# Moving the query chains of batches 4 and 5 to earlier half steps in a hand-ordered attention and highway kernel

## The chip, the cores and the metric

The kernel runs on one core of one Trainium2 chip. The metric is the time of one execution in device microseconds. Executions of one kernel differ by up to about 1 us either way.

Engines: PE is TensorE (PEld its weight loads), DVE VectorE, ACT ScalarE, POOL GpSimd, SP the engine that issues the transfers. L64 means line 64 of the kernel; L64 and L69 are helpers that issue all matmuls and all PE transposes, so groups are told apart by their tile names: `pq` query transposes, `psk` the kv product, `px` the attention output, `pt` and `ph` the two highway products, `nat` the output transposes. On the other engines `eq` and `ek` are the exps of queries and keys, `r` their sums and reciprocals, `qsT` the copied-out query transposes, `kvn` the normalised kv product (the "kv norm"), `dd` and `g` DVE's two steps of the highway layer, and `o` the output copies.

## The reference

Linear attention over 8 batches of 8 heads, 576 rows, 64 columns, followed by a highway layer on 512 columns:

```python
q_s = softmax(q, axis=-1)                    # over the 64 columns
k_s = softmax(k, axis=2)                     # over the 576 rows
kv  = einsum('bhsd,bhse->bhde', k_s, v)
x   = einsum('bhsd,bhde->bhse', q_s, kv)     # then heads side by side: 4608 x 512
H, T = relu(x @ w_h), sigmoid(x @ w_t + b_t)
out  = T * H + (1 - T) * x
```

## The kernel before

All instructions are issued by hand in one global order. Each engine executes its own instructions in that order, and in the traces a waiting instruction holds up those behind it: POOL of the kernel before idles 4.02 us in front of a scaling (57.79) though the data of the value casts behind it had landed by 53.0. The order is written as events at "half steps": `at(p, f)` puts `f` at position `p`, and the sorted events are emitted. Eight half steps make a slot. In the slot of batch b (it begins at p = 8(b-1)) the query chain of batch b ends on PE, while the highway layer of the batch before runs, one gate (`pt`) and one carry (`ph`) for each of four column blocks ("ob 0" to "ob 3"); chunk 2 is batch 2's highway work, and so on.

```python
def q_sums(b, a):                      # DVE: row sums of half a batch, 1152 elements a partition
    ...
    nc.vector.reduce_sum(qsum[b][:, :, h], eq[b][:, :, h, :], axis=AX.X)

def q_scale_p(b, n0, n1):              # POOL: exp times reciprocal of the sums
    e, r = eq[b][:, n0:n1], qsum[b][:, n0:n1]
    nc.gpsimd.tensor_mul(e, e, r.broadcast_to(list(e.shape)))

def q_trans(b, g, home=None):          # PE transposes into one PSUM bank, DVE copies out
    ...
    if home is None:
        home = ps_1.tile([P, 1024], FP16, tag="q1", name=f"pq_{b}_{g}")   # ps_1: a pool of one
    ...
    nc.vector.tensor_copy(qsT[b][:, :, n0:n1, :], t[:, :, 0:w, :])

# ... in the event list, for each batch b:
at(p + e0, E(exp_half, b, "q", 0))     # ACT
at(p + e1, E(exp_half, b, "q", 1))
at(p + s0, E(q_sums, b, 0))            # DVE
at(p + s1, E(q_sums, b, 1), E(q_recip, b))
at(p + sc, E(q_scale_p, b, 0, 4))      # POOL
```

A query's path is ACT (exp), DVE (sums, reciprocal), POOL (scaling), PE (transposes), DVE (copy `qsT`). And the second transpose of a batch cannot start before DVE has copied out the first, because the pool `ps_1` has one bank: in the kernel before, DVE's copy of batch 3's first starts at 50.78 and takes 0.69 us, and PE's second follows at 51.60.

The softmax here doesn't subtract the row's maximum and nothing guards it: scores larger than these inputs give would overflow.

## Time and profile before

| what | value |
|---|---|
| time, median of 3 runs | 132.03 us (132.03 to 132.52) |
| span of the profiled execution | 130.2 us |
| slot of batch 3, by first gate activations on ACT (45.90 to 57.53) | 11.6 us |
| slots of batches 4 and 5 | 12.6 and 13.3 us |
| slots of batches 6 and 7 | 11.2 and 10.5 us |
| PE stands in front of batch 4's second transpose | 0.81 us |
| PE stands in front of batch 5's first and third transpose | 0.92 and 0.78 us |

The last two rows of the table are from PE's timeline. Its columns are start, duration, engine, line, operation, output and input, count, and in brackets the idle time before it and what ended it:

```profile
62.04 0.62 PE L69 MATMUL pq<-ident,eq 128*128 128x128 f16 x8 [0.81 <-POOL eq L264]
71.06 0.62 PE L69 MATMUL pq<-ident,eq 128*128 128x128 f16 x8 [0.92 <-POOL eq L264]
74.97 0.27 PE L69 MATMUL pq<-ident,eq 128*128 128x128 f16 x2 [0.78 <-DVE qsT L282]
```

Twice PE waits for POOL's scaled queries, once for DVE's copy. Those stalls are what the change aims at. The stages and the chain are shown inside the prediction.

### The profile page before, as it was taken

How to read it: one execution, taken by the hardware profiler on the slowest of the kernel's cores; microseconds unless marked ns; L12 is line 12 of the kernel's file. 1: busy time of each engine (PE TensorE's matmuls, PEld its weight loads, DVE VectorE, ACT ScalarE, POOL GpSimd, SP SyncE). 2: the span in 40 equal slices, each digit the busy share in tenths (PEclk: the TensorE clock that was granted, in tenths of full speed). 3: DMA queues.
4: the chain of work that ended last, by engine and by line, in shares of the span. 5: the costliest groups of instructions: out<-in, count | busy, mean ns of one | idle time of the engine just before them, and what ended most of it. 6: DMA issues, size and time to landing. Idle time of an engine off the chain costs nothing.

```text
span 130.2 us, 3374 instructions
## 1 busy us (share of the span) xinstructions
PE 112.3 (86%) x1375; PEld 61.3 (47%) x1375; DVE 97.6 (75%) x179; ACT 92.6 (71%) x130; POOL 75.3 (58%) x71
## 2 busy tenths in 40 slices
PE   4999996986877999998997899989999999999810
PEld 1335442462334356444644464445555554788700
DVE  1396537797899999899698889769956566789920
ACT  3652159985998589779889956997994856657420
POOL 2006506790299999529947952994799535425400
PEclk9999999999999999999999999999999999999985
DMA  4999999999999999999999999999048406074991
GB/s 147 359 393 399 404 403 408 411 414 412 402 414 408 403 414 410 403 413 400 324 409 407 340 322 413 396 134 374 8 81 222 206 40 287 0 322 204 403 340 31
DMA packets 20584, 41.25 MB, mean 317 GB/s; under 512 B 5460, under 2 KB 5976, under 8 KB 19544
## 3 DMA queue, kind: packets, MB, share of 16 engines
q1 hardware_dynamic: 20568, 41.03, 84.6%
q8 instruction: 11, 0.18, 0.5%
q14 instruction: 5, 0.04, 0.1%
HBM read 30.41 MB, written 9.44 MB: 306 GB/s over the span
## 4 chain that ended last, share of the span: by engine, by line
PE 29%; DVE 20%; POOL 19%; DMA 11%; issue 7%; ACT 6%; SPq 3%; POOLq 0%; DVEq 0%; ACTq 0%
POOL eq L264 12%; DMA q<-in_q_dram 11%; PE ph L64 10%; PE pt L64 8%; DVE r L234 5%; DVE dd L401 5%; PE nat L64 4%; DVE g L409 4%; POOL g L420 4%; POOL v L195 3%; PE pq L69 3%; ACT eq L183 2%; SPq L96 2%; PE psk L64 2%; ACT w16h L116 1%
## 5 line engine op out<-in xcount | busy, mean ns | idle before, releaser
L264 POOL TENSOR_TENSOR eq<-eq,r 128x1024 f16<-128x1024 f16 (+2 forms) x16 | 29.8, 1876 | 15.2 <-DVE r L252 10.6
L64 PE MATMUL pt<-xT,w16t 128*128 128x512 f16 x128 | 34.0, 379 | 2.1 <-DVE dd L401 1.2
L64 PE MATMUL ph<-xT,w16h 128*128 128x512 f16 x128 | 33.4, 380 | 1.2 <-ACT w16h L116 0.8
L383 ACT ACTIVATE pt<-pt,bt 128x512 f32<-128x512 f32 (+1 forms) x40 | 24.7, 621 | 9.8 <-PE pt L64 9.3
L409 DVE SCALAR_TENSOR_TENSOR g<-pt,dd 128x512 f16<-128x512 f32 (+1 forms) x40 | 25.2, 633 | 3.4 <-DVE dd L401 0.5
L401 DVE SCALAR_TENSOR_TENSOR dd<-xT,ph 128x512 f16<-128x512 f16 x32 | 21.7, 679 | 6.4 <-PE ph L64 6.3
L420 POOL TENSOR_TENSOR g<-g,xT 128x512 f16<-128x512 f16 x19 | 21.7, 1157 | 5.7 <-DVE g L409 5.7
L64 PEld LDWEIGHTS <-w16t 128*128 128x128 f16 x160 | 14.8, 98 | 18.1 <-issue 5.2
L183 ACT ACTIVATE eq<-q 128x1152 f16<-128x1152 f32 x16 | 18.4, 1172 | 4.0 <-DMA q<-in_q_dram 4.0
L234 DVE TENSOR_REDUCE r<-eq 128x18 f32<-128x1152 f16 x12 | 16.2, 1346 | 4.6 <-ACT eq L183 4.5
L183 ACT ACTIVATE ek<-k 128x1152 f16<-128x1152 f32 x16 | 18.6, 1175 | 1.3 <-DMA k<-in_k_dram 1.3
L64 PEld LDWEIGHTS <-w16h 128*128 128x128 f16 x160 | 13.6, 98 | 11.6 <-ACT w16h L116 2.5
L195 POOL CAST v<-v 128x1152 f16<-128x1152 f32 x12 | 13.5, 1150 | 9.5 <-DMA v<-in_v_dram 9.5
L64 PE MATMUL nat<-ident,g 128*128 128x128 f16 x142 | 16.9, 219 | 1.2 <-ACT o L460 0.6
L64 PEld LDWEIGHTS <-g 128*128 128x128 f16 x144 | 13.2, 98 | 8.2 <-DVE g L409 1.1
L460 ACT COPY o<-nat 128x512 f32<-128x512 f32 x26 | 15.6, 601 | 0.0
L64 PE MATMUL warm<-wide,ident 128*128 128x512 f16 x41 | 12.2, 445 | 1.8 <-DVE wide L153 1.8
L354 ACT CAST xT<-px 128x1024 f16<-128x1024 f32 x10 | 10.2, 1017 | 4.9 <-PE px L64 4.9
L69 PE MATMUL pq<-ident,eq 128*128 128x128 f16 x104 | 8.5, 219 | 4.2 <-POOL eq L264 1.7
L282 DVE COPY qsT<-pq 128x1024 f16<-128x1024 f16 (+1 forms) x16 | 9.3, 588 | 1.9 <-PE pq L69 1.4
L69 PEld LDWEIGHTS <-eq 128*128 128x128 f16 x108 | 6.7, 97 | 7.7 <-POOL eq L264 2.6
L357 ACT CAST xT<-px 128x512 f16<-128x512 f32 x8 | 4.3, 591 | 8.2 <-PE px L64 8.2
(57 smaller groups left out, 107.8 us busy)
## 6 DMA issues: line engine op xcount, KB each, us to landing
out_dram<-o SPq DMA_DIRECT2D x8, 1024.0 KB, 4.8
q<-in_q_dram SPq DMA_DIRECT2D x7, 1152.0 KB, 13.5
k<-in_k_dram SPq DMA_DIRECT2D x7, 1152.0 KB, 13.2
v<-in_v_dram SPq DMA_DIRECT2D x5, 1152.0 KB, 13.8
v<-in_v_dram SPq DMA_DIRECT2D x6, 576.0 KB, 11.6
q<-in_q_dram SPq DMA_DIRECT2D x2, 576.0 KB, 3.9
k<-in_k_dram SPq DMA_DIRECT2D x2, 576.0 KB, 6.6
w32t<-in_moe_w_t_dram SPq DMA_DIRECT2D x1, 1024.0 KB, 10.3
```

Of the source, the lines that this page charges most:

```text
L64: mm = lambda o, l, r, st, sp: nc.tensor.matmul(o, l, r, start=st, stop=sp, skip_group_check=True)
L69: nc.tensor.matmul(o, i, ident, is_transpose=True, start=True, stop=True, skip_group_check=True,)
L183: nc.scalar.activation(dst[b][:, :, 2 * a : 2 * a + 2, :], in32[which][b][:, 2 * a : 2 * a + 2].rearrange("p c n d -> p n c d"), AF.Exp,)
L195: (eng or nc.gpsimd).tensor_copy(o, i)
L234: nc.vector.reduce_sum(qsum[b][:, :, h], eq[b][:, :, h, :], axis=AX.X)
L264: nc.gpsimd.tensor_mul(e, e, r.broadcast_to(list(e.shape)))
L354: copy[how](dst, t2.rearrange("p c (n d) -> p c n d", d=64))
L383: nc.scalar.activation(ps, ps, AF.Tanh, bias=bt2[:, ob : ob + 1], scale=0.5)
L401: nc.vector.scalar_tensor_tensor(dd, xv(ob), -0.5, ps, op0=ALU.mult, op1=ALU.max)
L409: nc.vector.scalar_tensor_tensor(gv(ob), th, 1.0, dd, op0=ALU.add, op1=ALU.mult)
L420: eng.tensor_add(gv(ob), gv(ob), xv(ob))
L460: nc.scalar.copy(o, flat(t))
```

## The change

The intent: the slots of batches 4 and 5 are longer than the later ones, and their query chains are placed later. So give them the later slots' half steps, let the scaled queries be ready sooner, and move the key exps, value casts, transposes, kv and x products to match. No operation is added or removed. The whole diff:

```diff
         if b > 2:
             e0, e1, s0, s1, sc = {
                 3: (-2.6, -1.6, -1.1, -0.1, 1),
-                4: (-5.5, -4.5, -2.8, -1.5, -1.4),
-                5: (-5, -4, -3.4, -2.7, -2.6),
-            }.get(b, (-6.6, -5.2, -5.5, -3.95, -3.9))
+                4: (-5.6, -4.4, -4.6, -3.0, -2.9),
+            }.get(b, (-6.6, -5.2, -5.4, -3.95, -3.9))
             at(p + e0, E(exp_half, b, "q", 0))
             at(p + e1, E(exp_half, b, "q", 1))
             at(p + s0, E(q_sums, b, 0))
             at(p + s1, E(q_sums, b, 1), E(q_recip, b))
             at(p + sc, E(q_scale_p, b, 0, 4))
-            at(p + sc + (0.5 if b > 5 else 0), E(q_scale_p, b, 4, N9))
-            s = p + (0 if b < 5 else -0.5)
+            at(p + sc + (0.5 if b > 4 else 0), E(q_scale_p, b, 4, N9))
+            s = p + (0 if b < 4 else -0.5)
             at(s, E(exp_half, b, "k", 0))
             at(s + 1, E(exp_half, b, "k", 1))
-            s = p + {3: 0, 4: 0, 5: 0.4}.get(b, -0.9)
+            s = p + (0 if b < 4 else -0.9)
             at(s, E(cast_v, b, 0))
-            at(s + (0.9 if b < 5 else 0), E(cast_v, b, 1))
+            at(s + (0.9 if b < 4 else 0), E(cast_v, b, 1))
         tr, kv, x = {
             2: ((5, 6, 7.1), (4, 6.2), (6.5, 7.2)),
             3: ((4, 4.9, 4.95), (4, 4), (5.9, 6.9)),
-            4: ((2.5, 3.9, 4.4), (4.5, 4.5), (5.9, 6.9)),
-        }.get(b, ((0.9, 2, 2.9), (4, 4), (5, 6)))
+            4: ((0.9, 1.9, 2.8), (4, 4), (5, 6)),
+        }.get(b, ((0.5, 1.5, 2.4), (4, 4), (5, 6)))
```

## The prediction

The sum came to +1.90 + 0.17 - 0.81 = +1.26 us, and 132.03 + 1.26 gives the 133.3 us. What the trace shows: a sum moves 1.27 us of DVE, it took 1.35 us with POOL idle and 1.34 with POOL busy, and the granted clock was 1.00 in all five stages.

> **What bounds the kernel now.** I read the page first, then the busy time by stage, then the chain that ended last in order of time, and at the end the timelines of DVE, ACT and PE around the places the chain names.
>
> ```profile
> span 130.2 us, 3374 instructions
> PE 112.3 (86%) x1375; PEld 61.3 (47%) x1375; DVE 97.6 (75%) x179; ACT 92.6 (71%) x130; POOL 75.3 (58%) x71
> POOL eq L264 12%; DMA q<-in_q_dram 11%; PE ph L64 10%; PE pt L64 8%; DVE r L234 5%; DVE dd L401 5%; PE nat L64 4%; DVE g L409 4%; POOL g L420 4%; POOL v L195 3%; PE pq L69 3%; ACT eq L183 2%; SPq L96 2%; PE psk L64 2%; ACT w16h L116 1%
> ```
>
> No engine is full, and the end is set by a path that hops between them: the query chain of a batch (exp on ACT, row sums and reciprocal on DVE, scaling on POOL, transpose on PE) is the largest named part of it. By stage, one row for each eight half steps, cut where the first gate activation of a chunk starts on ACT (slots of batches 3, 4, 5, 6, 7):
>
> ```profile
> core 0: us, PE busy (x) PEld busy (x) DVE busy (x) ACT busy (x) POOL busy (x), PEclk, DMA share, GB/s
> 45.90:57.50 11.60, 11.42 (x167) 6.37 (x166) 10.89 (x19) 10.07 (x13) 7.87 (x6) 1.00 1.04 410
> 57.50:70.10 12.60, 11.75 (x168) 6.58 (x165) 11.10 (x20) 11.62 (x15) 9.61 (x7) 1.00 1.02 385
> 70.10:83.40 13.30, 11.56 (x164) 6.65 (x164) 11.49 (x19) 10.65 (x15) 9.31 (x7) 1.00 1.01 369
> 83.40:94.60 11.20, 10.48 (x147) 5.49 (x145) 9.03 (x15) 10.48 (x15) 8.48 (x7) 1.00 0.72 192
> 94.60:105.10 10.50, 10.20 (x144) 5.36 (x142) 6.36 (x12) 7.57 (x13) 8.19 (x7) 1.00 0.54 158
> ```
>
> The slots of batches 4 and 5 last 12.6 and 13.3 us with PE busy 11.75 and 11.56: 0.85 + 1.74 = 2.6 us of PE idle, the most that the change could win. But look at the first row: in batch 3's slot DVE is busy 10.89 of 11.60 and PE 11.42. That slot has nothing to give, and the change puts work earlier into it. The chain there:
>
> ```profile
> 51.60 0.63 PE pq L69 x8
> 53.40 0.69 DVE dd L401
> 55.95 1.27 DVE r L234
> 57.24 0.39 DVE r L252
> 57.79 4.20 POOL eq L264 x2
> 62.04 0.62 PE pq L69 x8
> 63.97 0.76 PE psk L64 x72
> 68.55 0.39 DVE r L252
> 69.10 1.91 POOL eq L264
> ```
>
> The reader sees that batch 4's scaling (57.79) waits for DVE's second sum and reciprocal, and its second transpose (62.04) for that scaling. The timelines of ACT (first line) and DVE just before:
>
> ```profile
> 49.64 1.18 ACT L183 ACTIVATE eq<-q 128x1152 f16<-128x1152 f32 x1
> 49.34 0.68 DVE L401 SCALAR_TENSOR_TENSOR dd<-xT,ph 128x512 f16<-128x512 f16 x1
> 50.13 0.69 DVE L409 SCALAR_TENSOR_TENSOR g<-pt,dd 128x512 f16<-128x512 f32 x1
> 50.78 0.69 DVE L282 COPY qsT<-pq 128x1024 f16<-128x1024 f16 x1
> 54.01 1.35 DVE L234 TENSOR_REDUCE r<-eq 128x18 f32<-128x1152 f16 x1
> ```
>
> Batch 4's first query exp ends at 49.64 + 1.18 = 50.82. Batch 3's transpose copy qsT runs at 50.78, and PE's second transpose of batch 3 (51.60) can only start after it, as all transposes without a home of their own share one PSUM bank.
>
> [...] This trace agrees that a waiting head stops what stands behind it: POOL idles 4.02 us before 57.79 though the value casts behind it had their data (v of batch 4, issued 38.15, landed after 14.8 us, at 53.0). [...] the trace has 1.27 from start to next start, so moving a sum moves 1.27 us of DVE. [...] the trace agrees (1.35 us at 54.01 with POOL idle, 1.34 at 65.32 with POOL busy), so I add no contention. [...] The trace grants 1.00 in all five stages; [...] so I add no clock loss.
>
> **The change part by part.** Nothing is added or removed; only order changes. I compared the compiled order of both kernels on each engine.
>
> *Slot of batch 3.* Batch 4's first sum moves from behind dd 2 to ahead of g 1 and of batch 3's first qsT copy. Its input comes at 50.82, DVE is free at 49.95, so DVE stands 0.9 us and the sum runs about 50.85 to 52.12. g 1 (0.65) then ends at 52.77, qsT (0.69) at 53.46, and PE's second transpose starts near 53.50 in place of 51.60: **+1.90**. PE has finished kv (51.46) and has nothing in front of that transpose, so it idles 2 us. What follows on PE (last transpose, ph, px, pt, nat) follows in its old distances, so the first gate of the next chunk goes from 57.53 to about 59.43. What is bought: the second sum and reciprocal pass ahead of g 2. ph 2 starts 54.24, dd 2 ends 55.90, sum to 57.19, reciprocal to 57.60, POOL's scaling at about 57.75, against 57.79. So the query chain in absolute time stays where it was; it is the half steps around it that went 1.9 us later. "Sooner" by 1.5 half steps is consumed whole.
>
> *Slot of batch 4.* The scaling ends near 62.0 as before, so the second transpose starts near 62.0. Before, PE had by then done ph and pt of ob 1, and did pt of ob 2 next; now pt 1, nat, ph 1 (0.87 + 0.34 + 0.87 = 2.08) are still to come, so kv of batch 4 goes from 63.90 to about 65.97. From there to batch 5's reciprocal it took 5.03 us (to 68.93); one sum (1.27) now lies before kv and one dd (0.60) behind the reciprocal: 5.03 - 1.87 = 3.16, so 69.13, **+0.2**. The first gate of the next chunk follows kv by its old distance: 70.10 + 2.07 = 72.2. The key exps and casts of this slot cause no wait before (casts of batch 4 ended 64.17, with kv begun 63.90), and none after.
>
> *Slot of batch 5.* Scaling of batch 5 starts 69.25. Its second part now stands behind a gate addition (1.11 to next start): 69.25 + 1.86 + 1.11 + 2.28 = 74.5, against 69.10 + 4.14 = 73.24. The second transpose starts 74.55, not 73.58, then pt 1, nat, last transpose, ph 1, pt 2, nat up to kv: the old 62.04 to 63.90 distance, 1.86, plus 2.08 = 3.94, so kv of batch 5 at 78.5 against 77.23: **+1.26**. Here the change does win back 0.8 us: the stall on the qsT copy (0.78 before 74.97) has gone. DVE keeps up: kvn ends about 80.2, when PE gets to px.
>
> *Slots of batches 6 and 7.* The reciprocal of batch 6 goes from 80.42 to about 81.75, and orders are as before. The chain is unbroken from there (ACT 84.01, sum 86.77 and 90.06, scaling 94.93, casts 97.16, kv 99.45), with no slack to swallow the shift, nor anything to enlarge it. Sum: +1.90 (slot 3) + 0.17 (slot 4) - 0.81 (slot 5) = **+1.26 us**. 132.03 + 1.26 = **133.3 us**.
>
> **The rivals.** *The intended gain.* If the first sum did not stand in front of qsT, batches 4 and 5 would become like the later slots and up to 2.6 us of PE idle would go: 129.4 to 131. For it: the later slots run so, at 11.2 and 10.5 us. Against it: these have no PE transposes or qsT copies on DVE (9.03 and 6.36 busy, against 11), and the compiled order puts the sum first, with its data visibly late. *A transfer becomes the bound.* DMA moves about 400 GB/s until 85 us, so loads could be late for earlier exps. q of batch 5 was issued 40.05 and landed after 16.1 us (56.2), its exp comes at 62; v of batch 5 landed 61.8, its cast is due after 74. The outputs that stand ahead of the loads of batches 6 and 7 are issued 2 us later, which moves q of batch 7 from 79.8 to about 81, before its exp at 87. So a transfer is hidden both ways; were it not, 134 to 135. *The shift grows.* If DVE, 11 us busy per slot, never regains a PE gap in slot 5, the end is +2.1, 134.1. *The shift is swallowed* by a wait downstream that I read as rigid: 132.0 to 132.6.
>
> **Range and chances.** Centre 133.3; the swallowed case gives the low end 132.2 and the growing case the high end 134.5. Faster by over 2% means under 129.4, which only the full intended gain reaches: 0.03. Slower by over 2% means above 134.7, twice my sum: 0.09. Within 2%: 0.88.
>
> **What would show it.** In the changed kernel: DVE idle of 0.9 us before a sum near 50.8, released by ACT's query exp; PE idle of about 2 us before batch 3's second transpose, at 53.5, released by the qsT copy; POOL's scaling of batch 4 still at 57.6 to 57.9; the first gates of chunks 3, 4 and 5 near 59.4, 72.2 and 84.7; the slot of batch 5 shorter than before by about 0.8. I am wrong if that second transpose starts at 51.6, if the scaling of batch 4 starts a microsecond or more earlier, or if exps or casts wait for loads.

## The result, and the profile after

The changed kernel took 133.44 us (median of 4 runs, 133.09 to 133.69), against 132.03 us (median of 4, 131.69 to 132.52). The ratio is 1.0102, with a 95% interval of 1.0063 to 1.0141: slower by one per cent, clear of the noise. Ratios here are the mean time of one kernel's fast runs over that of the other's in the same rounds, so they are not quite the ratios of the medians that I quote. Executions over 1.5% slower than the fastest of the same kernel are left out of the means.

Stages of the changed kernel, cut at the same events as in the prediction (columns as there):

```profile
46.60:60.30 13.70, 11.67 (x170) 6.58 (x166) 12.22 (x22) 11.03 (x15) 9.77 (x8) 1.00 1.02 402
60.30:72.80 12.50, 11.60 (x166) 6.60 (x167) 10.65 (x18) 10.63 (x16) 8.48 (x6) 1.00 0.88 321
72.80:85.40 12.60, 11.40 (x163) 6.35 (x161) 10.57 (x18) 10.59 (x16) 8.58 (x7) 1.00 1.00 362
85.40:96.60 11.20, 10.48 (x146) 5.47 (x144) 9.03 (x15) 10.48 (x16) 8.50 (x7) 1.00 0.78 219
96.60:107.00 10.40, 10.12 (x142) 5.33 (x141) 6.27 (x12) 7.48 (x13) 8.10 (x7) 1.00 0.55 159
```

Batch 3's slot grew from 11.6 to 13.7 us, batch 4's stayed, batch 5's shrank from 13.3 to 12.6, and the rest is as before. DVE of the changed kernel at the place in question:

```profile
50.03 0.68 DVE L401 SCALAR_TENSOR_TENSOR dd<-xT,ph 128x512 f16<-128x512 f16 x1
51.53 1.35 DVE L234 TENSOR_REDUCE r<-eq 128x18 f32<-128x1152 f16 x1 [0.82 <-ACT eq L183]
52.80 0.68 DVE L409 SCALAR_TENSOR_TENSOR g<-pt,dd 128x512 f16<-128x512 f32 x1
53.40 0.68 DVE L282 COPY qsT<-pq 128x1024 f16<-128x1024 f16 x1
```

The first sum of batch 4 now stands in front of the first copy of batch 3. DVE idles 0.82 us for its data and then works 1.27 us on it before the two older instructions get their turn. PE's stalls in the changed kernel:

```profile
54.13 0.61 PE L69 MATMUL pq<-ident,eq 128*128 128x128 f16 x8 [1.99 <-DVE qsT L282]
62.65 0.62 PE L69 MATMUL pq<-ident,eq 128*128 128x128 f16 x8 [0.81 <-POOL eq L264]
75.26 0.62 PE L69 MATMUL pq<-ident,eq 128*128 128x128 f16 x8 [1.16 <-POOL eq L264]
```

And POOL's scalings in it, both parts of batch 4 in one line, then the two of batch 5:

```profile
58.40 4.19 POOL L264 TENSOR_TENSOR eq<-eq,r 128x1024 f16<-128x1024 f16 x2 [3.63 <-ACT o L460]
69.90 1.90 POOL L264 TENSOR_TENSOR eq<-eq,r 128x1024 f16<-128x1024 f16 x1 [4.02 <-ACT xT L354]
72.88 2.32 POOL L264 TENSOR_TENSOR eq<-eq,r 128x1280 f16<-128x1280 f16 x1
```

There is a new stall of 1.99 us on the copy. To compare start times, subtract the offset of the execution: the first gate activation of chunk 2 on ACT, ahead of everything the change moves, is at 45.90 before and 46.58 after, so 0.68 us. Then the scaling of batch 4 starts at 57.72 (before: 57.79) and that of batch 5 at 69.22 (69.10). The query chains that were to be sooner are where they were. (The names behind POOL's waits, `ACT o` and `ACT xT`, had come last by a hair; both times DVE's reciprocal ended 0.2 us before too, as DVE's timeline shows.)

In the same way, and with the offset removed, I read three marks in every kernel below: the start of kv of batch 4 (before: 63.90), of kv of batch 5 (77.23), and the first gate activation of chunk 7 (105.07). In the changed kernel they come **+1.99, +1.27 and +1.24 us** later.

### The profile page after: what moved, and what is told of

Read it like the earlier page. It is cut to its first block, busy times and chain, and to the rows that moved or that the text cites. A ratio compares the mean times of both kernels' runs of the same rounds, so it can differ in the third digit from the quotient of the medians.

```text
span 131.9 us, 3374 instructions
## 1 busy us (share of the span) xinstructions
PE 111.8 (85%) x1375; PEld 61.2 (46%) x1375; DVE 98.1 (74%) x179; ACT 92.3 (70%) x130; POOL 74.9 (57%) x71
## 4 chain that ended last, share of the span: by engine, by line
PE 30%; DVE 23%; POOL 11%; ACT 10%; DMA 8%; SPq 7%; issue 6%; DVEq 0%; POOLq 0%; ACTq 0%
PE ph L64 10%; PE pt L64 9%; DMA w32h<-in_moe_w_h_dram 8%; POOL eq L264 8%; DVE g L409 6%; DVE dd L401 5%; DVE r L234 4%; PE nat L64 4%; SPq L96 4%; SPq L111 3%; ACT eq L183 3%; PE pq L69 3%; PE psk L64 2%; DVE qsT L282 2%; ACT ek L183 2%
## 6 DMA issues: line engine op xcount, KB each, us to landing
v<-in_v_dram SPq DMA_DIRECT2D x6, 576.0 KB, 11.6
```

## The experiments

Each was run with a profile, all but the change itself with five rounds of timing beside the kernel before, and all gave correct results. The marks come from one profiled execution of each kernel; those of a6 and a8 were slow ones (see there). Medians are over all executions, ratios over fast ones. The marks' shifts against the kernel before, in us:

| run | median, us | ratio (95% interval) | kv 4 | kv 5 | gate of chunk 7 |
|---|---|---|---|---|---|
| the change | 133.44 | 1.0102 (1.006 to 1.014) | +1.99 | +1.27 | +1.24 |
| b1_casts_keys_only | 132.18 | 0.9997 (0.994 to 1.005) | +0.01 | +0.01 | -0.01 |
| b2_sums4_only | 132.51 | 1.0073 (1.004 to 1.011) | +0.85 | +0.83 | +0.80 |
| b3_turns4_only | 134.36 | 1.0200 (1.016 to 1.024) | +2.70 | +2.68 | +2.65 |
| a1_sums4_back | 133.75 | 1.0138 (1.009 to 1.019) | +2.74 | +2.03 | +2.00 |
| a2_turns4_back | 133.86 | 1.0042 (0.996 to 1.012) | +1.81 | +0.91 | +0.89 |
| a3_scale5_whole | 132.78 | 1.0070 (1.002 to 1.012) | +2.13 | +0.42 | +0.60 |
| a4_batch4_back | 131.09 | 0.9921 (0.988 to 0.997) | +0.65 | -0.25 | -0.27 |
| a6_sum4_behind_copy | 131.94 | 0.9978 (0.993 to 1.003) | +0.92 | +0.21 | +0.19 |
| a9_exp4_sooner | 132.49 | 1.0027 (0.997 to 1.008) | +1.26 | +0.54 | +0.51 |
| a8_sums5_behind_kv4 | 131.28 | 0.9918 (0.986 to 0.998) | 0.00 | -0.57 | -0.59 |
| a7_sum4_behind_copy_scale5_whole | 130.98 | 0.9934 (0.990 to 0.997) | +0.92 | -0.91 | -0.95 |

Names that begin with a are edits of the changed kernel, with b of the kernel before. The theory at the start was: batch 4's first sum blocks batch 3's copy on DVE, and batch 4's transposes, moved ahead of an unchanged scaling, make PE wait there. The rivals: only one of the two matters, or something else does (the key exps and casts, a transfer, ACT or DVE as the bound).

### Each half of the change by itself: undoing the sums

```diff
-                4: (-5.6, -4.4, -4.6, -3.0, -2.9),
+                4: (-5.6, -4.4, -2.8, -1.5, -1.4),
```

> Batch 4's sums, reciprocal and scaling go back to their old half steps; its transposes and all else stay as changed. My theory: batch 3's slot gets its 1.9 us back (second transpose about 1.9 us after the first's end is gone, no DVE wait for the query exp), but the scaling of batch 4 still ends about 62.0 us (in the time base of before) and PE reaches the second transpose of batch 4 two groups early, so the stall in front of it grows from 0.81 to about 2.7 us and kv of batch 4 stays 2 us late: about 133.3 us, +1.0% on before. Rival: the sum that stands in front of the transpose copy is the whole cost, so its removal gives 1.9 us back: about 131.5 us.

The rival fell at once: 1.0138, not 0.996. With the sum out of the way batch 3's slot is short again, and PE arrives at batch 4's transposes so early that it stands there: 1.92 us in front of the first one, where I had expected 2.7 us in front of the second. The time did not come back, it moved. The profile held a surprise. PE's timeline in a1:

```profile
60.51 1.01 PE L69 MATMUL pq<-ident,eq 128*128 128x128 f16 x8 [1.92 <-POOL eq L264]
61.30 1.91 PE L64 MATMUL ph<-xT,w16h 128*128 128x512 f16 x4
```

And stretches of time in a1 (length, busy time of the engines, and third from the right the granted clock):

```profile
58.00:60.50 2.50, 0.59 (x8) 0.32 (x5) 1.93 (x4) 2.50 (x4) 1.95 (x2) 1.00 0.88 346
60.50:62.00 1.50, 1.49 (x10) 1.11 (x11) 0.45 (x1) 1.35 (x2) 1.50 (x1) 0.53 1.10 425
63.00:64.00 1.00, 1.00 (x10) 0.99 (x9) 0.69 (x1) 0.00 (x0) 1.00 (x2) 0.51 1.16 262
64.00:65.00 1.00, 1.00 (x9) 0.52 (x8) 0.89 (x2) 0.01 (x1) 0.92 (x1) 1.00 0.78 286
```

After the stall PE's granted clock was 0.50 to 0.53 from 60.5 to 64 us: eight transposes took 1.01 us in place of 0.62, four `ph` matmuls 1.91 in place of 1.03. This is why kv of batch 4 came 2.74 us late in this profile and not the 2 us that I had worked out. That a1 is slower than the change itself is not shown: their intervals overlap. Nor does every execution have the half clock: 3.5 us of it would take about 0.013 off the mean clock (half of 3.5 us, in 132 us: my estimate), and two of a1's six executions had mean clocks of 0.989 and 0.990. They took 133.57 and 133.15 us, still over a microsecond more than the kernel before (132.06 in these rounds).

### Undoing the transposes

```diff
-            4: ((0.9, 1.9, 2.8), (4, 4), (5, 6)),
+            4: ((2.5, 3.9, 4.4), (4.5, 4.5), (5.9, 6.9)),
```

> Only batch 4's transposes, kv and x go back to their old half steps; its sums stay early. My theory: the 1.9 us stall of batch 3's second transpose stays, the stall before batch 4's second transpose (0.81) vanishes, but batch 5's early first sum now delays batch 4's second copy by about 0.9 us, so kv of batch 4 is still about 1.9 us late: about 133.2 us. Rival: the early transposes alone cost the time, the sums nothing: about 132.0 us.

Three of six executions were slow (134.2 to 134.4 us, clock 0.972 to 0.976), so the ratio rests on three fast ones (132.02, 133.04, 133.56) and its interval covers 1. The trace is clearer. The 1.99 us stall is there, the one before batch 4's second transpose is gone, and kv of batch 4 is still 1.81 us late, since batch 5's early sum delays batch 4's copy (PE stands 0.80 us for it, and 1.01 us more before `px`, as in a4 below). I expected 1.9 there. The end came 0.89 late where I expected about 1.2; the measured value lies between theory and rival, with the kv 4 mark on the theory's side.

### Doing one part alone

```diff
# b2, in the kernel before
-                4: (-5.5, -4.5, -2.8, -1.5, -1.4),
+                4: (-5.6, -4.4, -4.6, -3.0, -2.9),
# b3, in the kernel before
-            4: ((2.5, 3.9, 4.4), (4.5, 4.5), (5.9, 6.9)),
+            4: ((0.9, 1.9, 2.8), (4, 4), (5, 6)),
```

> The kernel before with only batch 4's sums and scaling moved as the change moves them (query exps by a tenth). My theory: batch 3's second transpose waits 1.9 us, batch 4's scaling starts at the same time as before, PE then reaches batch 4's second transpose after its data, so the old stall of 0.81 there vanishes, and kv of batches 4 and 5 and the end come about 1.1 us later: 133.1 us, ratio 1.008. Rival (the full cost is in the sum's stall): about 1.9 us later, 1.0145.

> The kernel before with only batch 4's transposes, kv and x moved as the change moves them. My theory: batch 3's slot is as before, but PE reaches batch 4's transposes before their scaling is done and stands about 2.8 us in two stalls (about 1.9 before the first, 0.9 before the second, in place of 0.81); kv of batches 4 and 5 and the end about 2.0 us later: 134.0 us, ratio 1.015, more by up to 1 us in executions where the stall brings the half clock that one such profile showed. Rival (the early transposes cost nothing where the sums are not late): no change, 132.0 us, 1.000.

The longest stall on PE in b2:

```profile
52.83 0.61 PE L69 MATMUL pq<-ident,eq 128*128 128x128 f16 x8 [1.99 <-DVE qsT L282]
```

And in b3:

```profile
60.17 1.04 PE L69 MATMUL pq<-ident,eq 128*128 128x128 f16 x8 [1.92 <-POOL eq L264]
```

b2 has the same 1.99 us stall as the change, but costs 0.8 to 0.85 us at the marks: the old 0.81 us in front of batch 4's second transpose has been absorbed. So it is 1.99 less 0.81, less 0.3 more that I had not accounted for; about half of that is a gap that stood there before too, since batch 3's second transpose starts 1.85 us later than before (53.45 against 51.60) and not 1.99. b3 has no stall on batch 3's copy and is the slowest of all, +2.7 us, with the halved clock again (0.50 to 0.56 from 60 to 63 us, transposes at 1.04 us). The half clock is not the whole of it: one of its executions, with a mean clock of 0.994, too high to hold it, took 133.83 us, 2.0 us over the kernel before (131.82). The two parts alone cost 0.85 and 2.70, and the change, which has both, 1.99: they do not add, because a stall caused by one is time in which the other's data arrives. (The change also has batch 5's part; batch 4's two parts together without it were not run.)

### Key exps and casts alone

```diff
# in the kernel before
-            s = p + (0 if b < 5 else -0.5)
+            s = p + (0 if b < 4 else -0.5)
-            s = p + {3: 0, 4: 0, 5: 0.4}.get(b, -0.9)
+            s = p + (0 if b < 4 else -0.9)
-            at(s + (0.9 if b < 5 else 0), E(cast_v, b, 1))
+            at(s + (0.9 if b < 4 else 0), E(cast_v, b, 1))
```

> The kernel before with only the key exps and value casts of batches 4 and 5 moved as the change moves them. My theory: neither is waited for, and the first key exp of batch 4 only fills ACT's idle time before the first gate activation of chunk 3: within 0.3 us of before, ratio 0.998 to 1.003. Rival: the key exp in front of the gate activation delays the blend and with it a PSUM bank: 0.5 us or more slower, 1.004 and up.

No shift at any mark. The first gate activation of chunk 3 does come 0.28 us later behind the key exp, as the rival said, but the stall before batch 4's second transpose (0.80) takes that up. In the kernel before, the key exps and casts alone are worth nothing that the marks or the times (0.5% either way) can show.

### What in DVE's order costs the 2 us

```diff
# a6: the sum behind the copy
-                4: (-5.6, -4.4, -4.6, -3.0, -2.9),
+                4: (-5.6, -4.4, -3.95, -3.0, -2.9),
# a9: the exp that the sum waits for, one place sooner on ACT
-                4: (-5.6, -4.4, -4.6, -3.0, -2.9),
+                4: (-6.1, -4.4, -4.6, -3.0, -2.9),
```

> As changed, but batch 4's first sum stands behind batch 3's first transpose copy and kv norm, instead of ahead of them. My theory: the copy runs where it did before the change, the 1.99 us stall before batch 3's second transpose falls to nearly none, dd 2 is about 1.0 us sooner than in the changed kernel, batch 4's scaling starts about 1 us sooner than in either kernel, kv of batch 4 about 1.0 us later than before the change (now 2.0) and the end about 0.2 us later: about 132.2 us, ratio to before 1.000 to 1.004. Rival: the stall came from something else, such as PE's own order or the load of the queries, and the time stays at 133.4 us, 1.010.

> As changed, but batch 4's first query exp goes ahead of the gate activation of ob 1 on ACT, one place sooner, so that its data is there when DVE reaches the sum. My theory: of the 1.99 us stall 0.8 us is DVE's wait for this exp and 1.2 us the length of the sum itself; the wait goes, the stall falls to about 1.1 us, part of it moves to the output transposes that wait for the later ACT copy (up to 1 us), and batch 4's scaling starts up to 1 us sooner: kv of batch 4 about 1.0 to 1.5 us later than before the change, end 132.3 to 132.8 us, ratio 1.002 to 1.006. Rival: only the length counts, no change from 133.4 us, 1.010.

DVE in a6:

```profile
51.82 0.69 DVE L282 COPY qsT<-pq 128x1024 f16<-128x1024 f16 x1
53.12 1.34 DVE L234 TENSOR_REDUCE r<-eq 128x18 f32<-128x1152 f16 x1
54.38 0.68 DVE L282 COPY qsT<-pq 128x1024 f16<-128x1024 f16 x1
```

The sum on DVE in a9:

```profile
50.87 1.34 DVE L234 TENSOR_REDUCE r<-eq 128x18 f32<-128x1152 f16 x1
```

And PE's new stall in a9:

```profile
51.78 0.27 PE L64 MATMUL nat<-ident,g 128*128 128x128 f16 x2 [0.91 <-ACT o L460]
```

And PE's new stall in a6:

```profile
55.31 0.22 PE L64 MATMUL px_l<-qsT,kvn 64*64 64x64 f16 x2 [0.90 <-DVE qsT L282]
```

The profiled execution of a6 was a slow one (133.24 us); its clock was 0.7 to 0.8 in the two slices of its page from 9.9 to 16.4 us, ahead of the marks, then 0.9 or more up to 128 us, and 1.00 from 48 to 68 us. In a6 the copy comes first, the stall before batch 3's second transpose is gone, and one of 0.90 us before `px` takes its place, because the sum now delays the second copy. The net is what was expected: kv of batch 4 +0.92 (expected 1.0), the end +0.19 (expected 0.2). In a9 the sum follows the `dd` before it at once, without idle time; 0.91 us of PE waiting appears in front of the output transposes, whose PSUM bank ACT empties later. That also is as expected, and the end is 0.73 us better than in the change. So the stall consists of a wait for data and of the sum's own length. The wait can be taken out (a9); the length can be moved behind the copy (a6), where most of it comes back as the 0.90 us.

### Batch 5's part

```diff
# a3
-            at(p + sc + (0.5 if b > 4 else 0), E(q_scale_p, b, 4, N9))
+            at(p + sc + (0.5 if b > 5 else 0), E(q_scale_p, b, 4, N9))
# a4: the edits of a1 and a2 together
-                4: (-5.6, -4.4, -4.6, -3.0, -2.9),
+                4: (-5.6, -4.4, -2.8, -1.5, -1.4),
-            4: ((0.9, 1.9, 2.8), (4, 4), (5, 6)),
+            4: ((2.5, 3.9, 4.4), (4.5, 4.5), (5.9, 6.9)),
```

> As changed, but both parts of batch 5's scaling stand together again on POOL, with the gate addition behind. My theory: the second part ends 1.1 us sooner, the stall of 1.16 us before batch 5's second transpose goes nearly to zero, everything after is about 1.0 us sooner: about 132.3 us, +0.2% on before. Rival: DVE or ACT is the bound of that slot and the time stays at 133.4 us.

> Both sums and transposes of batch 4 go back, only the key exps and casts of batch 4 and the changes of batch 5 stay. My theory: either of the two early moves of batch 4 costs about 2 us by itself and they overlap, so only undoing both gives it back: about 132.0 us, level with before, no win since batch 5's gain (reciprocal about 1.1 us sooner) is eaten by the gate addition inside its scaling. Rival: the two costs add up, so that this run and the two with one move undone differ by equal steps; or batch 5's part is a loss by itself: 132.5 us or more.

a3 has the sign and nearly the size: kv of batch 5 comes 0.85 us sooner than in the change, and no PE idle worth a record stands before batch 5's second transpose any more. (The profiled execution of a3 had a clock of 0.95 from 40 to 110 us, and four `ph` took 1.06 us in it for 1.03, so its marks may be a little late. By times a3 and the change are not apart: 1.002 to 1.012 and 1.006 to 1.014.) The gate addition that the change put between the halves of batch 5's scaling costs most of a microsecond in the profiles; a7 below shows 1.1 us for the same edit, at full clock.

a4 was better than I expected, 0.992 and not 1.000. The line that explains it:

```profile
66.60 0.22 PE L64 MATMUL px_l<-qsT,kvn 64*64 64x64 f16 x2 [1.01 <-DVE kvn L223]
```

With batch 4's kv back at its later half step, *both* sums of batch 5 stand ahead of batch 4's kv norm on DVE. That makes the norm late (PE stands 1.01 us) but puts batch 5's scaling 2.4 us sooner, and PE never waits for batch 5's transposes. I had counted on only 1.1 us sooner.

a4's marks cannot be set beside the others as they stand. Its profile has a stall that no other one has, before batch 3's second transpose:

```profile
51.61 0.62 PE L69 MATMUL pq<-ident,eq 128*128 128x128 f16 x8 [0.86 <-POOL eq L264]
```

In this execution POOL's work was already 0.72 us late at the zero point, before anything that a4's edits move (batch 3's scaling starts 2.17 us after it and not 1.45). That puts the transpose 0.72 us late and accounts for the +0.65 at kv of batch 4. By estimate all three marks would be some 0.7 us sooner without it, the last near -1.0, which agrees with the times (0.992 is 1.0 us) where -0.27 does not.

### Two versions that are faster than both kernels

```diff
# a8: a3 and a4, and both sums of batch 5 behind batch 4's kv norm
+                5: (-6.6, -5.2, -3.4, -3.35, -3.3),
# a7: a3 and a6 together
```

> The version with batch 4's sums and transposes back (0.992 of before), in which batch 5's first sum made DVE late for the kv norm of batch 4 (PE stalled 1.01 us before px). Here both sums of batch 5 stand behind that kv norm, and its scaling is whole. My theory: that stall goes, batch 5's scaling starts about 0.6 us sooner than before the change, and kv of batch 5 comes about 0.6 us sooner: 131.2 us or less, ratio 0.989 to 0.995. Rival: the sums' later start makes batch 5's scaling the bound again and the gain over before is gone: 132.0 us, 1.000.

> As changed, with batch 4's first sum behind batch 3's first transpose copy and kv norm, and batch 5's scaling whole. My theory: the first edit took 1.06 us off kv of batch 5 by the profiles, the second 0.85, and they lie one behind the other, so kv of batch 5 and the end come about 0.6 us sooner than before the change: 131.4 us, ratio 0.993 to 0.998. Rival: the two are worth the same wait and do not add: 132.2 us, 1.001.

Both intervals lie below 1. a8 has the shift that was worked out (-0.57 to -0.59 for -0.6); two of its six executions, the profiled one among them, were slow, and its marks are read from that slow execution, in which the clock was under 0.9 (0.7 to 0.8) only in the two slices of the page from 23.3 to 29.9 us, ahead of the marks, and in the last one. a7, -0.95 us at the last mark by its trace and 0.9934 by its times, adds a3's gain to a6's, and more: a6 still had a stall of 1.17 us before batch 5's second transpose, and all of it went, so that kv of batch 5 is 1.12 us sooner than in a6. What remains in it before batch 5's transposes is nothing; before batch 4's:

```profile
61.50 0.62 PE L69 MATMUL pq<-ident,eq 128*128 128x128 f16 x8 [0.79 <-POOL eq L264]
```

a7, a8 and a4 lie within each other's intervals; which of them is best is not settled.

## Why the prediction was right or wrong

The forecast of 133.3 us met 133.44. Its steps, with the 0.68 us offset removed from what was measured:

- *Batch 3's slot.* Second transpose at 53.50, measured 53.45; DVE's wait 0.9, measured 0.82; scaling of batch 4 at 57.75, measured 57.72; first gate of the next chunk near 59.43, measured 59.58. The key exp of batch 4, which now stands ahead of that activation on ACT, is the small rest, and I left it out of this step: PE's product ends at 59.96, ACT leaves the exp at 60.26, and b1 has the same 0.28 us.
- *Batch 4's slot.* kv 65.97, measured 65.89; scaling of batch 5 at 69.25, measured 69.22. The stall that stayed was 0.81, to the hundredth the old one.
- *Batch 5's slot.* Second transpose 74.55, measured 74.58; kv 78.5, measured 78.50. The old 0.78 stall on the copy is gone, the 1.16 on the scaling is new, as said. But the prediction puts the 0.81 down to the 0.78 stall alone, and that these two agree is luck: the 0.92 before the first transpose, which it does not name, went too, so 1.70 us of stalls went and 1.16 came. The measured gain is 0.72 (from +1.99 to +1.27); what lies between it and 0.54 I did not trace.
- *The later slots are rigid.* +1.27 at kv of batch 5 and +1.24 at chunk 7's first gate. The swallowed case and the growing case both failed.
- *Transfers are hidden.* No exp or cast of batches 4 to 7 waited for a load in the changed kernel: of the waits listed for its engines from 46 to 105 us of the trace, none ended with a transfer.

Two things in its reasoning were wrong or thinner than its result. First, the sum "+1.90 + 0.17 - 0.81" reads as if the sum on DVE were the cause of the loss and the rest were trifles. a1 and b3 show otherwise: without that stall the early transposes alone cost as much (a1) or more (b3). The 0.17 was small only because the 1.90 stood in front of it. Likewise its rival, that without the sum in front of the copy "up to 2.6 us of PE idle would go", was tested by a6: the stall went, and the time came level with before (0.998), not 1 to 2.6 us under it. Second, it added no clock loss for a PE gap of 2 us, which nothing in the trace of the kernel before shows: PE's longest wait there between 20 and 125 us is 1.25 us. It held in the changed kernel, whose granted clock was 1.00 in all five stages, and the stalls of 1.99 us in a2 and b2 and of 1.85 us in a3 had no such effect either (four `ph` behind them took 1.03 us, and 1.06 in a3 as ahead of its stall). But a stall of 1.92 us in the profiles of a1 and b3 was followed by half clock, 0.50 to 0.56, with PE busy 0.59 of 2.5 us in a1 against 0.14 of 2.1 us in the changed kernel. Two things differ, and no run here tells which of them decides, if either does. Transposes stand on both sides of the stall in a1 and b3 (3.1 us from the end of the last `pt` to the next `ph`), while the kv product stands before it in the others (2.5 to 2.7 us from its end to the next `ph`). And the stall's position in time: by their mean clocks, some executions of a1 and b3 did not have the half clock. The conclusion was right, the reason was not shown.

## What to carry to other kernels

On an engine that takes its work in order, as DVE does in these traces, "issue it sooner" means "put it ahead of something else": look at what then stands behind it, and when its data arrives, before counting the gain. Here a 1.27 us reduction, moved ahead of a copy with its data 0.82 us away, became a 1.99 us stall on PE and moved its own chain by 0.07 us. A chain is not sooner because its positions are; follow it to the one start time that matters (here POOL's scaling, 57.79 and 57.72). And when two moves belong together, try each alone as well as both: stalls overlap, so undoing one of two causes may return nothing (a1: 1.0138 against the change's 1.0102, by times not apart), or even cost (a1's profile: +2.74 us at kv of batch 4 against +1.99).
